# Background tasks cut into chains of small steps in an attention and gated-MLP kernel, with wo's splits and three sets of w_down's sums moved to chunk 1's projections

## The chip, the cores and the metric

The kernel runs on one core of one Trainium2 chip. The metric is the device time of one execution in microseconds; the time of the kernel before is the median of three runs. A profile of one more execution, with its trace, shows what each engine did: TensorE (PE, and PEld for its weight loads), VectorE (DVE), ScalarE (ACT), GpSimd (POOL) and SyncE (SP), whose in-order queue issues every DMA here.

## The reference

For x of 2048 x 1024, layer-normed to xn, the result is x + s * g. s is linear attention with learned feature maps and 32 heads of 32: phi is a pair of softmaxes (of p and of -p, with p = q w_phi or k w_phi), and

```python
kv = einsum("bhsf,bhsd->bhfd", phi_k, v)
z = einsum("bhsf->bhf", phi_k)
num = einsum("bhqf,bhfd->bhqd", phi_q, kv)
den = einsum("bhqf,bhf->bhq", phi_q, z)[..., None] + 1e-6
s = merge_heads(num / den) @ wo
g = silu((sigmoid(xn @ w_gate) * (xn @ w_up)) @ w_down)   # w_gate, w_up: 1024 x 3584
```

## The kernel before

Every large product is one level of a seven-product scheme on 2 x 2 blocks (names B11, T2, T3, B21, T1, T4, B22); the T operands are sums and differences of blocks, and results are formed by adding products in PSUM and in SBUF. Each operand is split into a high and a low part in the fast fp32 format (`split`: a ScalarE cast, L154, and a VectorE subtraction, L155), and each product is three matmuls (`mm3`, L159 to L161).

The 2048 rows go in two chunks of 1024. The stages, by the profile, are: chunk 0's projections V, K and Q (to about 300 us), chunk 0's GLU (to about 840), chunk 1's projections (to about 1078), chunk 1's GLU (to about 1650), the product with w_down (Down, to about 2170) and attention with wo (to the end). In a projection a group of four products (u = 0 to 3) goes to four banks, and `proj_out` evacuates them together. In the GLU there are 28 units of seven products, one bank each of 12 matmuls; the evacuations are L881 (B11, ScalarE), L883 (T2), L885 (T3), and L891 to L900 (B21, T1, T4, B22). Four banks go round; B21, T4 and B22 accumulate in the banks of B11, T3 and T1, so the evacuation of T3, say, must be over before T4 begins, one product later. In Down a step is eight banks of three matmuls (24 in all), 14 steps are one product of the scheme, and `evacuate` takes the eight banks at the end of it (L955 and L956 for B21, L973 for T4), through a ring `yr` of y buffers where the result is stored to g_d.

All else is background work, put between the products:

- `k_task(hb, t)`, 16 row tiles by 2 halves: load of k and v from qkv_d, `features` (row maxima and minima L451, L452, subtractions L460, L461, Exp L462, sums L464, reciprocal L465), L478, two splits, L489; then the products of phi and v (`kv_products`, L501). After each half come `kv_sum`, `kv_blocks` and `z_broadcast`.
- `q_features(t, hb)`: the same features for q, stored to e_d and r_d.
- `x_fetch`, `x_turn`: load, norm and transposition of chunk 1's rows.
- `wd_sums(j)`: four loads of w_down, four differences on POOL, four stores to wd_d (14 sets). `o_task(k)`: four loads of wo, four sums on POOL, seven splits stored to wo_d through three buffers (4 tasks).
- `q_task(t, hb)`, during Down: load of e_d (L635), multiplication by z on POOL, denominators on VectorE (L642 to L649), a second multiplication on POOL, four stores to f_d (L654). 32 tasks.

Each of these is one function that traces all its instructions at once. `background(anchor, tasks)` takes the next task from a queue; `tc.issue_after(anchor)` orders the task's instructions on the anchor's engine (VectorE, as the anchors are evacuations) behind the anchor. What lies on other engines is only ordered by the compiler's scheduler, which has priorities by program order. Where the tasks go is in the main loop: `bg_proj0` takes four k tasks beside Q of chunk 0, one per group; `bg_glu0` the rest of chunk 0's work at evenly spaced products (list `due`); `bg_proj1` six sets of sums beside V and K of chunk 1, and `late_k` five tasks beside its Q; `bg_glu1` all that is left, 25 of late_k's tasks, wo's four and eight sets of sums, and 16 q_features, mixed evenly over 188 products. In Down, 32 q_tasks are spread over 78 steps, and the loads of w_down's operands (L602) and of h_d (L608) are issued by `down_prep`.

Places in SBUF are numbered slots of two halves of 512 columns; 36 to 38 are block p, 43 to 46 block fb, 47 to 54 block fc.

## Time and profile before

| what | value |
|---|---|
| time, median of 3 runs | 2418.87 us (2418.68 to 2419.66) |
| time of the profiled execution | 2424.93 us |
| its span, first to last instruction | 2423.2 us |
| granted TensorE clock, mean | 0.995 |
| DVE, ACT, POOL busy | 67%, 41%, 50% |
| DMA, mean | 258 GB/s |

Busy times add up what each engine ran, and their shares are means over stages that differ. Matmuls are pipelined and their ends are modelled, so the number of matmuls in a stretch says more of TensorE's pace than its busy time does. A wait is put down to the event that came last before the waiting instruction started. Page lines such as "L885 DVE" name the line of the kernel; L154, L155 and L58 are helpers that many places call (L58 is POOL's piecewise sum, difference or product), and there the tile names tell the places apart (w, p, x, fb and so on; "stk" and "stq" are the small tiles of a k and a q task).

### The profile page before, as it was taken

Reading aid. Unit: us, or ns where it says so; the run is one execution under the profiler, and the core shown is the slowest. Engines: PE = TensorE matmul, PEld = TensorE weight load, DVE = VectorE, ACT = ScalarE, POOL = GpSimd, SP = SyncE. Lnnn points to the kernel's source line nnn. Section 1 sums busy time; section 2 is a strip of 40 time slices with the busy share of each in tenths; the row PEclk is TensorE's granted clock in tenths of the full one; section 3 lists DMA queues with packets and bytes.
Section 4 is the critical chain, followed back from the end, with each engine's and each line's share of the span. In section 5 each row is a group of like instructions: output and inputs, shape, how many; then the busy total and the mean of one; then the engine's idle time right before and its main releaser. Section 6 shows DMA issues by size and latency. Waiting matters only on the chain.

```text
span 2423.2 us, 32511 instructions
## 1 busy us (share of the span) xinstructions
PE 2356.5 (97%) x10728; PEld 1948.3 (80%) x10728; DVE 1630.7 (67%) x2341; ACT 1004.0 (41%) x1490; POOL 1212.1 (50%) x1394
## 2 busy tenths in 40 slices
PE   7999999999999999999999999999989999999998
PEld 5788887788888888888788777878878887888887
DVE  7434797677677764387857898765556675567775
ACT  6432354444454442235544454343333333345442
POOL 5630265867768463003434655353444545533766
PEclk9999999999999999999999999999999999999999
DMA  7775466888888698568898978788667766878664
GB/s 283 256 271 173 156 236 238 288 301 304 274 305 313 245 328 274 174 212 287 288 340 297 309 273 298 268 305 316 218 202 238 249 209 221 281 251 295 213 192 157
DMA packets 262329, 626.22 MB, mean 258 GB/s; under 512 B 37904, under 2 KB 58384, under 8 KB 257552
## 3 DMA queue, kind: packets, MB, share of 16 engines
q1 hardware_dynamic: 262160, 624.15, 74.8%
q8 instruction: 84, 1.38, 0.2%
q14 instruction: 85, 0.70, 0.1%
HBM read 374.47 MB, written 249.56 MB: 258 GB/s over the span
## 4 chain that ended last, share of the span: by engine, by line
PE 65%; DMA 9%; POOL 9%; DVE 8%; issue 6%; ACT 2%; SPq 1%; DVEq 0%; POOLq 0%; ACTq 0%
PE bank L159 21%; PE bank L160 21%; PE bank L161 21%; POOL fc L58 5%; POOL fb L58 2%; POOL x L58 1%; DMA wo_d<-p 1%; DMA fb<-w_down 1%; DVE w L155 1%; DVE p L155 1%; DMA out<-fc 1%; DMA fc<-e_d 1%; PE bank L501 1%; DMA wf_d<-x 1%; DMA f_d<-fc 1%
## 5 line engine op out<-in xcount | busy, mean ns | idle before, releaser
L159 PE MATMUL bank<-x,w 128*128 128x512 f32 x2352 | 910.3, 392 | 31.0 <-DVE fc L885 9.1
L160 PE MATMUL bank<-x,w 128*128 128x512 f32 x2352 | 918.0, 390 | 0.0
L161 PE MATMUL bank<-x,w 128*128 128x512 f32 x2352 | 909.6, 390 | 0.0
L58 POOL TENSOR_TENSOR fc<-fc 128x256 f32<-128x256 f32 x532 | 447.3, 871 | 598.5 <-DVE fc L900 217.2
L159 PEld LDWEIGHTS bank<-x,w 128*128 128x128 f32 x2352 | 442.8, 188 | 133.3 <-DVE fc L885 11.5
L155 DVE TENSOR_TENSOR w<-fa,w 128x512 fp32r<-128x512 f32 (+1 forms) x444 | 397.3, 898 | 225.1 <-ACT w L154 214.4
L161 PEld LDWEIGHTS bank<-x,w 128*128 128x128 f32 x2352 | 443.2, 188 | 93.2 <-DVE w L155 0.3
L160 PEld LDWEIGHTS bank<-x,w 128*128 128x128 f32 x2352 | 443.3, 188 | 90.7 <-DVE x L155 0.3
L154 ACT CAST w<-fa 128x512 fp32r<-128x512 f32 (+1 forms) x444 | 308.0, 698 | 487.2 <-PE bank L160 313.6
L159 PE MATMUL bank<-w,x 128*128 128x512 f32 x708 | 278.3, 393 | 6.3 <-ACT x L154 3.4
L161 PE MATMUL bank<-w,x 128*128 128x512 f32 x708 | 277.4, 393 | 2.9 <-DVE x L155 2.9
L160 PE MATMUL bank<-w,x 128*128 128x512 f32 x708 | 277.0, 391 | 0.0
L58 POOL TENSOR_TENSOR fb<-fa 128x256 f32<-128x256 f32 x112 | 104.8, 956 | 223.5 <-DMA fc<-qkv_d 131.4
L58 POOL TENSOR_TENSOR fb<-fb,fc 128x256 f32<-128x256 f32 x132 | 122.4, 947 | 186.7 <-DVE fc L900 186.5
L159 PEld LDWEIGHTS bank<-w,x 128*128 128x128 f32 x708 | 133.5, 189 | 36.1 <-ACT x L154 5.6
L161 PEld LDWEIGHTS bank<-w,x 128*128 128x128 f32 x708 | 133.5, 189 | 31.7 <-DVE x L155 4.8
L160 PEld LDWEIGHTS bank<-w,x 128*128 128x128 f32 x708 | 133.6, 189 | 26.7
L58 POOL TENSOR_TENSOR fb<-fb 128x256 f32<-128x256 f32 x116 | 111.7, 988 | 71.9 <-DMA fb<-w_down 35.6
L155 DVE TENSOR_TENSOR x<-fa,x 128x512 fp32r<-128x512 f32 x112 | 90.6, 809 | 76.9 <-ACT x L154 76.9
L154 ACT CAST w<-fb 128x512 fp32r<-128x512 f32 (+1 forms) x114 | 71.1, 625 | 130.3 <-PE bank L160 92.6
L154 ACT CAST x<-fa 128x512 fp32r<-128x512 f32 x112 | 69.5, 620 | 122.4 <-DMA fa<-wd_d 66.2
L58 POOL TENSOR_TENSOR fc<-fc,sa 128x256 f32<-128x256 f32 x128 | 105.6, 853 | 21.0 <-issue 20.1
(204 smaller groups left out, 2877.0 us busy)
## 6 DMA issues: line engine op xcount, KB each, us to landing
ws_d<-w SPq DMA_DIRECT2D x112, 512.0 KB, 4.4
w<-ws_d SPq DMA_DIRECT2D x112, 512.0 KB, 5.6
fa<-w_gu SPq DMA_DIRECT2D x84, 512.0 KB, 5.2
fa<-h_d SPq DMA_DIRECT2D x84, 512.0 KB, 5.2
fa<-wf_d SPq DMA_DIRECT2D x32, 1024.0 KB, 5.8
h_d<-fc SPq DMA_DIRECT2D x120, 256.0 KB, 4.2
h_d<-fb SPq DMA_DIRECT2D x76, 256.0 KB, 4.6
fc<-qkv_d SPq DMA_DIRECT2D x64, 256.0 KB, 4.6
```

Source lines behind the costliest of these rows:

```text
L58: self.engine.tensor_tensor(o[:, s], a[:, s], b[:, s], op=op)
L154: nc.scalar.copy(o[0], src)
L155: return nc.vector.tensor_sub(o[1], src, o[0].bitcast(F32))
L159: nc.tensor.matmul(o, a[0], b[0], start=first, stop=False, **kw)
L160: nc.tensor.matmul(o, a[0], b[1], start=False, stop=False, **kw)
L161: nc.tensor.matmul(o, a[1], b[0], start=False, stop=last, **kw)
L501: nc.tensor.matmul(kvb[g // 2][:, g % 2 * 256:g % 2 * 256 + 256], v[:, g].rearrange("p a f -> p (a f)"), ph[:, g].rearrange("p a f -> p (a ...
```

## The change

Each background function becomes a generator, with `yield` between its steps, and a class runs chains of them:

```diff
+class Steps:
+    def __init__(self, *tasks):
+        self.tasks, self.now = deque(tasks), None
+        self.left = self.total = sum(n for n, _ in tasks)
+    def step(self):
...
+        self.left -= 1
+        self.now[0] -= 1
+        over = next(self.now[1], self) is self
```

A k task is 8 steps, a q_features 5, an x task 7 (fetch and turn in one), a set of sums 2, a wo task 6, a q_task 5; kv_sum, kv_blocks and z_broadcast are 4, 6 and 5. In a k task, for example:

```diff
         nc.vector.tensor_reduce(mx, pv, axis=AX.X, op=ALU.max)
         nc.vector.tensor_reduce(mn, pv, axis=AX.X, op=ALU.min)
+        yield
...
         nc.vector.tensor_tensor(ev[:, 1], mn, pv, op=ALU.subtract)
         nc.scalar.activation(e, e, AF.Exp)
+        yield
+        if not query:
+            v = whole(38).rearrange("p (g a f) -> p g a f", g=8, a=2)
+            split((v[:, :, 0], v[:, :, 1]), vraw.rearrange("p (g f) -> p g f", g=8))
+        yield
```

The products of phi and v wait for one further call (`KV_WAIT = 1`). The small tiles of features get tags of their own for k and q, one buffer each in place of two shared. The tasks are dealt out anew:

```diff
+    early_k = Steps(*ks[:CTT])
+    late_k = Steps(*ks[CTT:])
+    p_again = (2, lambda: plain(block, "p", 36, 3, F32))
+    beside0 = Steps(*xs), Steps(p_again, *qs[:16])
+    beside1 = late_k, Steps(*wd[WD1:], *qs[16:])
+    proj1 = Steps(*os, *wd[:WD1])
-    def background(anchor, tasks):
+    def background(anchor, tasks, n=1):
         kv_products()
-        if tasks:
-            with tc.issue_after(anchor):
-                tasks.popleft()()
+        with tc.issue_after(anchor):
+            for _ in range(n):
+                tasks.step()
+
+    def paced(anchor, streams, products):
+        n = -(-sum(a.left for a in streams) // max(1, products))
+        for _ in range(n):
+            background(anchor, max(streams, key=lambda a: a.left / a.total))
```

with `WD1 = 3` in place of 6. In the projections, one step behind each of the four evacuations of a group:

```diff
             for u in range(4):
                 proj_out(c, what, i, u, pbank[u])
...
+                if c == 0 and what == Q:
+                    background(last_evac[0], early_k)
+                elif c and not (what == V and i in (B11, B21)):
+                    if what != Q and u < 3 and proj1.left:
+                        background(last_evac[0], proj1)
+                    elif what == Q and i not in (B11, B21):
+                        background(last_evac[0], late_k)
```

and in the GLU, for the product number m of a chunk (0 to 195), in place of the `due` lists:

```diff
+        if m > 1:
+            if c:
+                paced(v.ins, beside1, 191 - m)
+            elif early_k.left:
+                background(v.ins, early_k)
+            else:
+                kv_products()
+                paced(v.ins, beside0, 187 - m)
```

wo's tasks load into slots 47 and 52 (before: 43 and 44). In Down there are two streams of q_tasks, for even and odd t, each with its buffers (e in slot 50 or 51, the product with z in 52 or 47), one step of each behind each step's last split; the y ring gives up slot 47:

```diff
-    yr = Ring(halves(47, 48, 49))
+    yr = Ring(halves(48, 49))
...
+        e, ez = whole(50 + t % 2), whole((52, 47)[t % 2])
...
+    late = [Steps(*[(5, lambda t=t, hb=hb: q_task(t, hb)) for hb in range(2) for t in range(a, TT, 2)]) for a in range(2)]
...
+        if n < 2 * NJ * 3 - 2:
+            for a in range(2):
+                if late[a].left and (n or not a) and late[a].left > 5 * 16 * (80 - n) // 82 - 3 * a:
+                    with tc.issue_after(last_split[0]):
+                        late[a].step()
```

A q_task's steps are: the loads; the first multiplication; the denominators; the second multiplication; the stores to f_d.

More of the change, by code (lines that the diff above doesn't have):

```diff
@@ L39, in next @@
         return self.items[(self.n - 1) % len(self.items)]
+class Steps:
[3 more added lines that the diff above has]
+    def step(self):
+        if self.now is None:
+            if not self.tasks:
+                return
+            self.now = self.tasks.popleft()
+            self.now = [self.now[0], self.now[1]()]
+        self.left -= 1
+        self.now[0] -= 1
+        over = next(self.now[1], self) is self
+        assert over == (self.now[0] == 0)
+        if over:
+            self.now = None
 class Pieces:
@@ L298, in o_task @@
         pool.sub(a12, a12, a11)
[L299 to L300 removed]
+        yield
+        yield
+        keep(T2, a11)
+        keep(T3, a21)
+        yield
+        keep(T1, a22)
+        keep(B22, a12)
     o_r = Ring((36, 37, 38))
@@ L475, in k_task @@
         nc.sync.dma_start(vraw, qkv_d[V, t, hb])
-        r = features(f"k{t}{hb}", kraw, e_k)
+        yield
+        r = yield from features(f"k{t}{hb}", kraw, e_k)
+        yield
         e3 = e_k.rearrange("p (g d) -> p g d", d=DH)
@@ L491, in k_task, with kv_products @@
             nc.sync.dma_start(zk_d, zacc)
-        kv_due.append((t, ph, v))
+        kv_due.append([KV_WAIT, t, ph, v])
     kv_due = deque()
-    def kv_products():
+    KV_WAIT = 1
+    def kv_products(now=False):
         while kv_due:
-            t, ph, v = kv_due.popleft()
+            if not now and kv_due[0][0]:
+                kv_due[0][0] -= 1
+                return
+            _, t, ph, v = kv_due.popleft()
             for g in range(8):
@@ L628, in q_features @@
         nc.sync.dma_start(p, qkv_d[Q, t, hb])
-        r = features(f"q{t}{hb}", p, e, True)
+        yield
+        r = yield from features(f"q{t}{hb}", p, e, True)
         nc.sync.dma_start(r_d[t, hb], r)
@@ L982, in hedgehog_glu_kernel @@
     ND = len(dsteps)
-    late = [(t, hb) for hb in range(2) for n in range(CTT) for t in (2 * n, 2 * n + 1)]
+    late = [Steps(*[(5, lambda t=t, hb=hb: q_task(t, hb)) for hb in range(2) for t in range(a, TT, 2)]) for a in range(2)]
     for n, (i, j, cs) in enumerate(dsteps):
@@ L1004, in hedgehog_glu_kernel @@
         if n == 0:
-            assert not (bg_proj0 or bg_glu0 or bg_proj1 or bg_glu1 or kv_due)
-        if n and n * 32 // 78 > (n - 1) * 32 // 78 and late:
-            t, hb = late.pop(0)
-            if t == 0:
-                nc.sync.dma_start(zb, zb_d[hb])
-            with tc.issue_after(last_split[0]):
-                q_task(t, hb)
+            assert not any(a.left for a in (early_k, proj1, *beside0, *beside1)) and not kv_due
+        if n < 2 * NJ * 3 - 2:
[3 more added lines that the diff above has]
+                        late[a].step()
         if 40 <= n < 56 and n % 2 == 0:
@@ L1014, in hedgehog_glu_kernel @@
         if n == ND - 2 * NJ:
-            assert not late and len(WO[B21]) == 4
+            assert not any(a.left for a in late) and len(WO[B21]) == 4
             block("x1", 4, 4, F32R)
```

117 lines of the change are left out of this document (56 added, 61 removed).

## The prediction

> **What bounds the kernel now.** I read the page's busy totals first, then busy times by stretch (all matmuls, and those of L501 alone), then who waited for whom on TensorE, then the timelines around the longest waits. Columns of the stretches: length, busy time of PE, PEld, DVE, ACT and POOL with instruction counts, granted clock, DMA share, GB/s. The last three rows of the first fence are L501's alone.
>
> ```profile
> PE 2356.5 (97%) x10728; PEld 1948.3 (80%) x10728; DVE 1630.7 (67%) x2341; ACT 1004.0 (41%) x1490; POOL 1212.1 (50%) x1394
> 300.00:480.00 180.00, 174.93 (x782) 143.08 (x781) 143.68 (x201) 84.87 (x123) 126.91 (x131) 1.00 0.72 254
> 480.00:840.00 360.00, 360.00 (x1590) 298.10 (x1589) 259.32 (x389) 169.19 (x244) 254.36 (x299) 1.00 0.83 292
> 900.00:1020.00 120.00, 120.00 (x531) 99.37 (x530) 46.71 (x51) 32.38 (x39) 27.33 (x30) 1.00 0.70 239
> 1080.00:1650.00 570.00, 556.29 (x2508) 456.50 (x2507) 437.99 (x596) 265.04 (x360) 263.94 (x284) 1.00 0.85 299
> 1320.00:1500.00 180.00, 170.85 (x767) 138.50 (x767) 159.99 (x208) 84.24 (x104) 100.69 (x100) 0.99 0.84 290
> 1650.00:2170.00 520.00, 507.07 (x2212) 417.96 (x2211) 308.43 (x512) 180.07 (x310) 248.17 (x302) 0.99 0.72 239
> 300.00:480.00 180.00, 5.95 (x40) 5.37 (x40) 1.00 0.72 254
> 1080.00:1650.00 570.00, 24.86 (x176) 23.77 (x176) 1.00 0.85 299
> 1320.00:1500.00 180.00, 11.48 (x80) 10.68 (x80) 0.99 0.84 290
> ```
>
> TensorE is busy for 97% of the span, so only its lost time can be won. The undisturbed stretch 480 to 840 gives its pace: 360 us / 1590 = 0.2264 us from one matmul to the next. An L501 matmul (phi times v) has half the columns; its mean is 284 ns against 390, so I take 0.226 - 0.106 = 0.12 us.
>
> ```profile
> L160 PE MATMUL bank<-x,w 128*128 128x512 f32 x2352 | 918.0, 390 | 0.0
> L501 PE MATMUL bank<-p 128*128 128x256 f32 x256 | 36.4, 284 | 0.4 <-DVE p L155 0.3
> ```
>
> Lost time by stage is the length less the matmuls at that pace. Early in chunk 0's GLU (300 to 480): 180 - 742 x 0.2264 - 40 x 0.12 = **7.2 us**. Chunk 1's GLU (1080 to 1650): 570 - 2332 x 0.2264 - 176 x 0.12 = **21 us**. Down (1650 to 2170): 520 - 2212 x 0.2264 = **19.2 us**. Together 47 us; the opening and the last stage are not touched by the change. Who ended TensorE's waits in those three stages, in that order:
>
> ```profile
> PE bank L159 <- DVE fc L885: 3.6, 2, 2.3
> PE bank L159 <- DVE fc L885: 5.6, 4, 2.7
> PE bank L159 <- DVE fc L956: 6.8, 1, 6.8
> PE bank L159 <- DVE fc L973: 5.2, 1, 5.2
> ```
>
> All are VectorE evacuations of a bank that the next product needs. Why were they late? Rows of the timelines of VectorE, SyncE's queue and ScalarE around the long waits (start, length, then the idle time before it):
>
> ```profile
> 1382.12 1.21 DVE L461 TENSOR_TENSOR fc<-stk,fc 128x512 f32<-128x512 f32 x1
> 1383.25 0.67 DVE L885 TENSOR_TENSOR fc<-fc,bank 128x512 f32<-128x512 f32 x1
> ...
> 1469.61 1.22 DVE L464 TENSOR_REDUCE stk<-fc 128x32 f32<-128x1024 f32 x1 [2.46 <-ACT fc L462]
> 1470.75 0.68 DVE L885 TENSOR_TENSOR fc<-fc,bank 128x512 f32<-128x512 f32 x1
> ...
> 1804.48 1.78 SPq L654 DMA_DIRECT2D f_d<-fc  x4
> ...
> 1808.90 0.38 SPq L602 DMA_DIRECT2D fa<-wd_d  x1
> ...
> 1814.18 0.62 ACT L154 CAST x<-fa 128x512 fp32r<-128x512 f32 x1 [9.74 <-DMA fa<-wd_d]
> ...
> 2054.39 0.86 SPq L957 DMA_DIRECT2D g_d<-fc  x2
> 2060.38 1.35 DVE L973 TENSOR_TENSOR fc<-x,bank 128x512 f32<-128x512 f32 x2 [5.55 <-DMA g_d<-fc]
> ```
>
> At 1382 the last of a run of two background tasks' features stands in front of L885. At 1469 VectorE stands in its queue waiting for the task's Exp (L462), with L885 behind it. At 1804 f_d's stores, which need POOL's product, leave SyncE's in-order queue; the next task's load of e_d (L635) reuses their buffer and must wait for them to land, and wd_d's load (L602) stands behind it until 1808.90. ScalarE's queue then waits 9.74 us for that load, with the evacuation L955 behind the wait. At 2060 an evacuation waits for a y buffer whose store left at 2054.39.
>
> **The change part by part.**
>
> *Chunk 0.* The eight early k tasks become 64 steps: 28 places among Q's projections (four per product group) and 36 after GLU products, one each, where before there were whole tasks every fifth product. Nothing is added. A step puts at most two wide VectorE operations in front of an evacuation, about 2.3 us by the two 1.2 us rows above; a product lasts 12 x 0.2264 = 2.72 us and the evacuation 0.68, so a lone step rarely makes TensorE wait. After the Exp come other instructions before L464. Of 7.2 us I leave 1.5: **gain 5.7** (bounds 0 and 7.2). The products of phi and v come one call later (KV_WAIT), which nothing waits for before kv_sum. The 138 steps of x and q that follow are also one a product, in the stretch that lost nothing; they stay free.
>
> *Chunk 1's projections.* wo's four tasks (24 steps) and three sets of w_down's sums (6) take 30 of 36 places in V and K; before there were six sets of sums. New on VectorE and ScalarE there: 28 splits; on POOL, 4 tasks against 3 sets, nearly nothing; on SyncE's queue 24 MB in place of 12 (a task loads 1 MB and stores 3.5, a set moves 2). The fill row is 900 to 1020: VectorE 46.7 of 120 us, ScalarE 32.4, the DMA share 0.70. The splits cost here what they cost in the GLU now:
>
> ```profile
> L155 DVE TENSOR_TENSOR p<-fb,p 128x512 fp32r<-128x512 f32 x28 | 23.7, 859 | 21.0 <-ACT p L154 20.8
> ```
>
> 23.7 us beside an idle VectorE is hidden by TensorE's own work; without that cover it would cost all of it. Before these splits VectorE also stood 20.8 us for ScalarE's cast, 0.7 each, while three buffers go round to wo_d. Evacuations that queue behind such a wait have three other banks' time, 3 x 2.72 us, until TensorE needs theirs. The bounds are 0 and 20.8; near the bottom, **1.5 us lost**, as 900 to 1020 loses none now.
>
> *Chunk 1's GLU.* wo's splits leave (23.7 us of VectorE), but Q's places now take 20 k steps, 2.5 tasks, where five whole tasks went before, so 2.5 tasks more come here. Pacing changes more: 202 k steps and 102 others for 189 products, rounded up, is two steps a product for the first 115 and one for the last 74. Costs, summed over these rows:
>
> ```profile
> L489 DVE TENSOR_TENSOR fc<-fc 128x1024 f32<-128x1024 f32 x20 | 27.9, 1396 | 0.1
> L478 DVE TENSOR_TENSOR fc<-fc,stk 128x1024 f32<-128x1024 f32 x21 | 27.0, 1286 | 0.4
> L155 DVE TENSOR_TENSOR p<-fc,p 128x512 fp32r<-128x512 f32 (+1 forms) x51 | 52.6, 1032 | 6.2 <-ACT p L154 3.7 <-PE bank L543 2.3
> L464 DVE TENSOR_REDUCE stk<-fc 128x32 f32<-128x1024 f32 x21 | 25.5, 1215 | 15.5 <-ACT fc L462 15.5
> L461 DVE TENSOR_TENSOR fc<-stk,fc 128x512 f32<-128x512 f32 x21 | 18.2, 866 | 0.0
> L451 DVE TENSOR_REDUCE stk<-fc 128x16 f32<-128x512 f32 x20 | 13.5, 677 | 4.3 <-DMA r_d<-stq 2.9 <-DMA fc<-qkv_d 1.4
> ```
>
> (L461 stands for its twin L460 too, L451 for L452.) A k task: 1.40 + 1.29 + 2 x 1.03 + 1.22 + 2 x 0.87 + 2 x 0.68 = 9.1; neighbours overlap by 0.08 (1469.61 + 1.22 ends after 1470.75), ten of them: **8.3 us**, with a short reciprocal **8.5**. A q task is the features alone, L464 to L451 of these rows: 4.3, less overlap and with its reciprocal **4.1**. Foreground: five and a half evacuations of 0.6 (L885 above, less overlap) and three splits like wo's of 0.78 in seven products, 0.8 us a product. In the densest part (about products 52 to 117) two steps a product are 0.171 k and 0.13 q tasks: 1.45 + 0.53 + 0.8 = 2.8 us of VectorE a product, against 2.72 + 0.171 x 8 x 0.12 = 2.88 us of TensorE. So VectorE is filled to 97% there for some 190 us; then one step a product, about 60%. Now, 1320 to 1500 has 160 us of VectorE for 687 x 0.2264 + 80 x 0.12 = 165 us of matmuls, as dense, and loses 15 us in its lumps. Without lumps and waits on Exp I leave 9 us there and 3 for the 11 sets of sums that lead the list at once (before: 8, spread): **12 of 21, gain 9** (bounds: 18 gained, if only evacuations of the kind at 1469 mattered; 24 lost, below).
>
> *A page beside the trace.* The Trainium skill, "TensorE: Matmul & The Clock Gate", section "Part 1: The HAM clock gate", has the clock fall after an idle window of about 3.4 us, so by it the 2.7 us wait at 1469 costs only itself. The next row disagrees: the granted clock was 0.69 right behind it, 11 matmuls in 3.5 us where 15.5 fit, 1.0 us more. By the page the gain would be 1 us smaller.
>
> ```profile
> 1471.50:1475.00 3.50, 3.50 (x11) 2.79 (x12) 3.46 (x4) 1.94 (x3) 3.50 (x4) 0.69 1.04 409
> ```
>
> *Down.* A q task becomes five steps, one a down step (24 x 0.2264 = 5.4 us), in two streams with buffers of their own. f_d's stores are queued a step after the multiplication that they wait for, and e_d's next load a step after the stores. So what held SyncE at 1804 goes, and with it the 6.8 us and the slow matmuls behind it. The price: slot 47 goes to the second stream, and the y ring falls from six halves to four, so at B21 and T4 the fifth of eight evacuations waits for the first's store instead of the seventh. Unshown; bounds: nothing, if stores leave at once (TensorE needs bank 4 only 2.7 us into the next step), and the present 19 us again, if they still leave late. The store at 2054 was late because of f_d and e_d ahead of it, so I stand near the bottom: 5 us left, **gain 14**. A wait in VectorE's queue at L973, or in ScalarE's at L955, holds the splits of later steps behind it, which run some steps ahead of TensorE.
>
> Sum: 5.7 - 1.5 + 9 + 14 = **27 us**. The profiled execution took 2424.93 us (span 2423.2); the median is 2418.87, 6 us lower, and I take the gain off it unchanged: **2392 us**.
>
> **The rivals.**
>
> *The two-step stretch binds on VectorE (slower).* Beside POOL, two-input operations stretch:
>
> ```profile
> L461 DVE TENSOR_TENSOR fc<-stk,fc x32: 676/684/1222, 226.9 to 1581.7; 128x512 f32<-128x512 f32 x32
> L900 DVE TENSOR_TENSOR fc<-fc,bank 128x512 f32<-128x512 f32 x39 | 26.4, 678 | 19.3 <-PE bank L161 10.7 <-POOL fb L58 8.3
> ```
>
> At the long end (1.2 for each 0.7, in L460, L461, the splits and L489) a k task is 10.4, a q task 4.9, the foreground 0.96: 3.4 us a product, 0.5 over, for some 75 products: 37 us, with 8 elsewhere 45 in place of 21. Less 18 from the other stages: +6, **2425**. The point from which it is slower is (39 - 8) / 75 = 0.41 us a product over the 2.88. For it: the sums crowd at the front. Against: they end before much of the stretch. The Trainium skill, "SBUF — State Buffer", section "Who interferes with whom", says that a VectorE instruction with two SBUF inputs contends with a GpSimd instruction that reads SBUF, and one with a single SBUF input does not. L461's spread and L900's steady 678 ns (one input is a bank) agree.
>
> *The smaller ring keeps Down's loss.* The other gains stay: -13, **2406**. For it: the wait at 2060 was already one for the ring. Against: what made that store late goes.
>
> *The change doesn't do what it says.* Only a step's VectorE instructions are tied behind the product; ScalarE's, POOL's and the queue's are not, and steps may be compiled back to back. Lumps stay, ring and pacing eat what Down yields: **2418**.
>
> *Nearly all is recovered:* **2374**.
>
> **How the numbers follow.** Forecast 0.57 (its own range 2379 to 2408), smaller ring 0.14, VectorE binds 0.14, no effect 0.09, all recovered 0.06. The range leaves out most of the last and the upper half of the slower case: 2377 to 2421. A change within 0.2% (4.8 us) can't be told from none: faster 0.74, same 0.11, slower 0.15.
>
> **What would show it.** Right: L885 and L893 nearly gone from TensorE's waits, no wait behind L956; VectorE above 90% in about 1150 to 1420 and light afterwards. Wrong: TensorE losing more than 20 us there with VectorE full; L955 or L973 waiting for g_d; ScalarE's splits waiting for wo_d in 860 to 1000 with TensorE idle.

## The result, and the profile after

The kernel after takes **2398.81 us** (median of 4 runs, 2394.39 to 2404.23) against 2419.26 for the kernel before (4 runs, 2418.68 to 2420.41): a ratio of **0.9916, 95% interval 0.9894 to 0.9938**, 20.4 us less. Its profiled execution took 2404.23 us (span 2402.4), the slowest of its four; the span of the profiled execution before was 2423.2. So the two traces differ by 20.8 us. The four runs of the new kernel lie 10 us apart. Those of the kernel before lie 2 apart here, but 8 to 15 in the 11 to 23 runs beside each set of experiments. So a number read from one trace of either has to be held against a scatter of that size.

The line numbers have moved: `split` is L175/L176 (before L154/L155), `mm3` L180 to L182 (L159 to L161), POOL's helper L79 (L58), phi times v L547 (L501). In the GLU B11 is L954, T3 L958 (L885), B21 L964/L966 (L891/L893), L970 and L973 T1 to B22 (L897, L900); in Down B21 is L1020 (L956), T4 L1037 (L973). First the busy totals, then the stretches that the prediction used, all matmuls (the columns are those of the prediction).

```profile
PE 2348.1 (98%) x10728; PEld 1946.5 (81%) x10728; DVE 1632.3 (68%) x2341; ACT 1000.8 (42%) x1488; POOL 1201.5 (50%) x1394
...
300.00:480.00 180.00, 180.00 (x818) 149.99 (x817) 148.25 (x202) 88.37 (x128) 127.42 (x134) 1.00 0.72 256
480.00:840.00 360.00, 358.70 (x1580) 296.24 (x1580) 256.96 (x392) 171.16 (x244) 251.02 (x297) 1.00 0.83 291
900.00:1020.00 120.00, 120.00 (x531) 99.39 (x530) 56.72 (x68) 41.15 (x57) 40.61 (x48) 1.00 0.91 328
1080.00:1650.00 570.00, 554.49 (x2508) 455.80 (x2507) 430.07 (x575) 247.27 (x331) 260.44 (x280) 1.00 0.79 275
1650.00:2170.00 520.00, 518.79 (x2300) 429.66 (x2299) 322.43 (x538) 191.87 (x331) 251.85 (x305) 1.00 0.75 250
```

The work is the same: 10728 matmuls and 2341 VectorE instructions, as before. Early in chunk 0's GLU 818 matmuls run where 782 ran; in Down 2300 where 2212 ran. In chunk 1's GLU the number has not changed: 2508 and 2508.

The lost time of a stretch is reckoned as in the prediction: its length, less its matmuls at 0.2264 us, those of phi and v (L501, L547) at 0.12. For 300 to 480, for example, 180 - 770 x 0.2264 - 48 x 0.12 = -0.1 (48 of the 818 are L547's); a number within about 1 of zero means that nothing was lost, as whole matmuls are counted at the edges. In this table are all kernels of this study, microseconds lost in each stretch of one trace each, and the measured ratio to the kernel before on the same chip.

| kernel | 300 to 480 | 480 to 840 | 840 to 1080 | 1080 to 1200 | 1200 to 1440 | 1440 to 1680 | 1680 to 2160 | ratio (95% interval) |
|---|---|---|---|---|---|---|---|---|
| before | 7.2 | 0.0 | 0.1 | 1.7 | 11.1 | 7.5 | 19.0 | |
| after | -0.1 | 2.3 | 0.1 | 8.1 | 12.8 | -0.8 | 1.6 | 0.9916 (0.9894, 0.9938) |
| e1_lump_glu | 0.6 | 6.6 | -0.1 | 9.0 | 8.4 | 1.1 | 2.1 | 0.9944 (0.9931, 0.9956) |
| e2_lump_down | -0.1 | 4.8 | 0.1 | 3.8 | 10.5 | -0.9 | 4.3 | 0.9905 (0.9891, 0.9919) |
| e3_even | 0.0 | 2.3 | 3.1 | 8.4 | 7.4 | -0.6 | 4.1 | 0.9913 (0.9900, 0.9926) |
| e4_spread | -0.1 | 2.3 | -0.1 | 6.1 | 13.2 | 0.2 | 2.1 | 0.9904 (0.9887, 0.9922) |
| e5_even_spread | -0.1 | 3.2 | 2.4 | 6.1 | -0.5 | -0.9 | 3.0 | 0.9894 (0.9881, 0.9907) |
| e6_old_down | -0.1 | 2.5 | -0.1 | 6.1 | 10.7 | -0.9 | 18.8 | 0.9981 (0.9971, 0.9991) |
| e7_one_ez | 0.1 | 3.4 | 0.1 | 4.0 | 10.2 | -0.9 | 0.0 | 0.9912 (0.9898, 0.9927) |
| e8_wo_back | 0.0 | 1.8 | 0.1 | 0.3 | 19.5 | 11.0 | 1.2 | 0.9979 (0.9967, 0.9990) |
| e9_pairs | -0.1 | 2.7 | -0.1 | 6.5 | 10.7 | -0.8 | 3.2 | 0.9925 (0.9903, 0.9948) |
| e10_buffers | 0.0 | 2.3 | -0.1 | 3.3 | 10.7 | -0.7 | 27.7 | 1.0002 (0.9989, 1.0015) |
| e11_wo_back2 | 0.0 | 2.7 | -0.1 | 9.5 | 7.8 | 14.6 | 1.6 | 0.9989 (0.9970, 1.0008) |
| e12_all | 0.1 | 2.3 | 3.3 | 2.7 | 0.0 | -0.6 | 1.6 | 0.9883 (0.9861, 0.9906) |

From before to after: 7.3 won early in chunk 0's GLU and 2.3 lost later in it, nothing in the projections, 0.2 in chunk 1's GLU (20.3 and 20.1), 17.4 in Down. That is 22.6, beside the 20.8 between the spans.

Chunk 1's GLU has changed inside. Its three parts, before and then after:

```profile
1080.00:1200.00 120.00, 118.77 (x545) 97.70 (x544) 93.34 (x132) 62.93 (x89) 42.74 (x47) 1.00 0.80 282
1200.00:1440.00 240.00, 232.57 (x1042) 189.82 (x1041) 185.52 (x252) 113.01 (x147) 119.97 (x126) 1.00 0.88 311
1440.00:1650.00 210.00, 204.95 (x925) 168.98 (x925) 159.12 (x214) 89.10 (x124) 101.23 (x111) 0.99 0.84 294
```

```profile
1080.00:1200.00 120.00, 113.77 (x513) 92.68 (x512) 81.55 (x100) 40.87 (x56) 79.53 (x89) 1.00 0.90 316
1200.00:1440.00 240.00, 230.72 (x1045) 188.28 (x1044) 202.99 (x278) 115.65 (x150) 106.20 (x113) 1.00 0.81 279
1440.00:1650.00 210.00, 210.00 (x954) 174.84 (x953) 145.54 (x199) 90.75 (x126) 74.72 (x79) 1.00 0.71 246
```

The end of the stage is free now (954 matmuls for 925). The head is worse: POOL is busy for 79.53 us of 120 where it was busy for 42.74, and TensorE does 513 matmuls for 545. In the middle VectorE is busy for 203 of 240 us, 85%, and from 1264 on, to 1440, for 164.65 of 176 us, 94%. Next come the rows of who ended TensorE's waits in 1080 to 1440 (total, times, longest), and then what the three engines did around one place in the head: VectorE, POOL and ScalarE, each with the idle time before an instruction.

```profile
PE bank L547 <- DVE p L176: 3.2, 3, 1.8
PE bank L180 <- ACT fc L954: 3.0, 2, 1.7
PE bank L180 <- DVE fb L966: 2.5, 2, 1.8
PE bank L180 <- DVE fc L973: 2.3, 3, 1.4
PE bank L180 <- DMA w<-ws_d: 2.2, 2, 1.6
PE bank L180 <- ACT fb L964: 1.6, 1, 1.6
...
```

The largest row is not an evacuation: the products of phi and v (L547) wait for the splits of phi on VectorE. Up to 1200 the waits add up to 2.9 us behind ScalarE, 2.2 behind loads and 1.1 behind VectorE; from 1200 on they are 7.1 behind VectorE and 1.7 behind ScalarE.

```profile
1107.67 0.68 DVE L176 TENSOR_TENSOR w<-fa,w 128x512 fp32r<-128x512 f32 x1
1116.32 0.69 DVE L973 TENSOR_TENSOR fc<-fc,bank 128x512 f32<-128x512 f32 x1 [7.97 <-POOL fc L79]
```

```profile
1112.08 2.82 POOL L79 TENSOR_TENSOR fb<-fb 128x256 f32<-128x256 f32 x4 [1.54 <-DMA fb<-w_down]
1114.86 1.43 POOL L79 TENSOR_TENSOR fc<-fc 128x256 f32<-128x256 f32 x2
```

An evacuation at the head (L973, of T4) waits 7.97 us: it writes the buffer that POOL's product for T1 (L79, fc) still has to read, and that product ends at 1116.29. POOL had spent its time on w_down's sums (fb), for whose loads it waits in its queue. In 1080 to 1200 VectorE's waits for POOL add up to 18.4 us; in the kernel before they were 1.3. ScalarE has its own waits. The longest row of each in 1200 to 1440, after and then before:

```profile
ACT L497 <- DVE fc L496: 42.5, 9, 8.7
```

```profile
ACT w L154 <- PE bank L160: 23.5, 13, 3.4
```

After, ScalarE's Exp (L497) stands 42.5 us in its queue for VectorE's subtraction (L496), 44.7 with three short rows; before it was 23.7 (three rows, 11.1, 7.5 and 5.1). The evacuations L954 and L964, which appear among TensorE's waits above, are ScalarE's and come behind such waits, as its timeline in the head shows (1123.84 behind a cast, 1134.00 behind an Exp and the load of a table for the evacuation's sigmoid):

```profile
1122.89 1.04 ACT L175 CAST p<-fc 128x1024 fp32r<-128x1024 f32 x1 [8.19 <-DVE fc L520]
1123.84 0.58 ACT L954 COPY fc<-bank 128x512 f32<-128x512 f32 x1
...
1131.63 1.06 ACT L497 ACTIVATE fc<-fc 128x1024 f32<-128x1024 f32 x1 [6.68 <-DVE fc L496]
1132.71 1.28 ACT L964 ACT_TABLE_LOAD   x1
1134.00 0.60 ACT L964 ACTIVATE fb<-bank 128x512 f32<-128x512 f32 x1
```

Before, ScalarE's longest row was a wait for TensorE (the buffer of a split that a product still reads), which is a wait of an engine that is ahead.

### The profile page after: what moved, and what is told of

It reads as the page before. It is cut to its first block, busy times and chain, and to the rows that moved or that the text cites. A ratio compares the mean times of both kernels' runs of the same rounds, so it can differ in the third digit from the quotient of the medians.

```text
span 2402.4 us, 32573 instructions
## 1 busy us (share of the span) xinstructions
PE 2348.1 (98%) x10728; PEld 1946.5 (81%) x10728; DVE 1632.3 (68%) x2341; ACT 1000.8 (42%) x1488; POOL 1201.5 (50%) x1394
## 4 chain that ended last, share of the span: by engine, by line
PE 69%; DMA 10%; POOL 7%; DVE 6%; issue 5%; ACT 1%; SPq 0%; POOLq 0%; DVEq 0%; ACTq 0%
PE bank L180 23%; PE bank L181 23%; PE bank L182 23%; POOL fc L79 4%; POOL fb L79 2%; POOL x L79 2%; DMA fb<-w_down 1%; DMA r_d<-stq 1%; DMA fa<-w_down 1%; DMA wd_d<-fb 1%; PE bank L547 1%; DVE w L176 1%; DVE p L176 1%; DMA w<-ws_d 1%; DVE x L176 1%
## 5 line engine op out<-in xcount | busy, mean ns | idle before, releaser
L180 PE MATMUL bank<-x,w 128*128 128x512 f32 x2352 | 909.5, 391 | 14.7 <-DVE fb L966 3.8
L182 PE MATMUL bank<-x,w 128*128 128x512 f32 x2352 | 905.6, 390 | 0.0
L79 POOL TENSOR_TENSOR fc<-fc 128x256 f32<-128x256 f32 x540 | 466.8, 895 | 420.9 <-DMA fc<-e_d 110.6
L176 DVE TENSOR_TENSOR w<-fa,w 128x512 fp32r<-128x512 f32 (+1 forms) x444 | 395.3, 893 | 229.5 <-ACT w L175 207.8
L180 PEld LDWEIGHTS bank<-x,w 128*128 128x128 f32 x2352 | 441.5, 188 | 113.7 <-DVE fb L966 5.6
L175 ACT CAST w<-fa 128x512 fp32r<-128x512 f32 (+1 forms) x444 | 307.5, 698 | 507.0 <-PE bank L181 346.9
L182 PEld LDWEIGHTS bank<-x,w 128*128 128x128 f32 x2352 | 441.7, 188 | 91.6
L180 PE MATMUL bank<-w,x 128*128 128x512 f32 x708 | 278.9, 394 | 7.2 <-ACT x L175 4.3
L182 PE MATMUL bank<-w,x 128*128 128x512 f32 x708 | 278.2, 394 | 2.9 <-DVE x L176 2.9
L79 POOL TENSOR_TENSOR fb<-fb,fc 128x256 f32<-128x256 f32 x132 | 124.6, 964 | 196.4 <-DVE fc L973 195.8
L79 POOL TENSOR_TENSOR fb<-fa 128x256 f32<-128x256 f32 x112 | 99.8, 911 | 244.0 <-DMA fc<-qkv_d 129.5
L180 PEld LDWEIGHTS bank<-w,x 128*128 128x128 f32 x708 | 134.0, 189 | 36.7 <-ACT x L175 6.5
L182 PEld LDWEIGHTS bank<-w,x 128*128 128x128 f32 x708 | 133.8, 189 | 32.1 <-DVE x L176 4.8
L79 POOL TENSOR_TENSOR fb<-fb 128x256 f32<-128x256 f32 x108 | 96.5, 919 | 113.9 <-DMA fb<-w_down 109.2
L175 ACT CAST p<-fc 128x512 fp32r<-128x512 f32 x100 | 75.3, 757 | 168.2 <-DVE fc L520 78.1
L79 POOL TENSOR_TENSOR fc<-fc,sa 128x256 f32<-128x256 f32 x128 | 96.6, 784 | 97.3 <-issue 90.8
L176 DVE TENSOR_TENSOR x<-fa,x 128x512 fp32r<-128x512 f32 x112 | 94.4, 843 | 46.4 <-ACT x L175 46.2
L175 ACT CAST w<-fb 128x512 fp32r<-128x512 f32 (+1 forms) x114 | 71.1, 625 | 128.6 <-PE bank L181 90.2
```

The lines of the kernel that those rows point to most:

```text
L79: self.engine.tensor_tensor(o[:, s], a[:, s], b[:, s], op=op)
L175: nc.scalar.copy(o[0], src)
L176: return nc.vector.tensor_sub(o[1], src, o[0].bitcast(F32))
L180: nc.tensor.matmul(o, a[0], b[0], start=first, stop=False, **kw)
L182: nc.tensor.matmul(o, a[1], b[0], start=False, stop=last, **kw)
```

## The experiments

All kernels are the kernel after with the edit shown, and ran as it did, beside runs of the kernel before. Those had a median of 2421 to 2423 us there, not 2419.26, so ratios compare the kernels and times do so only roughly.

### Whole tasks in the GLU, at the new places

```diff
     def step(self):
...
+            if self.whole:
+                list(self.now[1])
+                self.now[1] = iter(range(self.now[0] - 1))
...
-    early_k = Steps(*ks[:CTT])
+    early_k = Steps(*ks[:CTT], whole=True)
```

and the same for late_k, both streams of chunk 0 and the second stream of chunk 1: each task is issued whole at the place of its first step, and its other places are empty.

> The changed kernel with its pacing, slots and streams, but each background task in the projections' Q places and both GLUs traced whole at the place of its first step (the places of its other steps stay empty); Down, and wo's splits beside chunk 1's projections, keep their steps. If small steps are what freed the evacuations in the GLUs (theory A), chunk 0's GLU loses about 7 us again in 300 to 480 and chunk 1's more than its 21, with L885's successor L958 and L966 long in TensorE's waits: some 10 to 20 us slower than the changed kernel, 2409 to 2419. If only where the tasks are put mattered (rival), it stays within 4 us of 2399.

Measured: 2410.04 us (2406.87 to 2413.59, 5 runs), ratio 0.9944 (0.9931, 0.9956). The two stretches of chunk 0's GLU:

```profile
300.00:480.00 180.00, 180.00 (x811) 149.05 (x810) 148.59 (x200) 87.72 (x127) 129.22 (x132) 1.00 0.73 254
480.00:840.00 360.00, 354.90 (x1561) 292.22 (x1560) 253.95 (x384) 161.49 (x236) 253.73 (x296) 1.00 0.82 289
```

Early in chunk 0's GLU 811 matmuls run, nearly as many as with steps (818) and far more than before (782). So it is not the smallness of the steps that frees this stretch. It is the new places, or another part of the change that this kernel keeps (KV_WAIT, the small tiles' own tags); these were not tried apart. Later, in 480 to 840, the lumps lose 6.6 us where the steps lose 2.3. In chunk 1's GLU they lose 18.5, no more than the kernel after in its own trace (20.1). The ratio lies 0.0028 higher than that of the kernel after, about 7 us, with intervals that just overlap; the trace places about 4 of it. By the ratio it comes to 2406 us, which lies between the two expectations.

### Down taken apart: steps, dealing, buffers

The change to Down has three parts: q_tasks in steps; the **dealing**, an even and an odd task begun right behind each other and then no new one for some steps, where before a whole task came every 2.44 steps; and a second buffer for the product with z, paid for by a y ring of four halves instead of six. Five kernels separate them.

Whole q_tasks at the new places, with the new buffers and ring:

```diff
-    late = [Steps(*[(5, lambda t=t, hb=hb: q_task(t, hb)) for hb in range(2) for t in range(a, TT, 2)]) for a in range(2)]
+    late = [Steps(*[(5, lambda t=t, hb=hb: q_task(t, hb)) for hb in range(2) for t in range(a, TT, 2)], whole=True) for a in range(2)]
```

> The changed kernel with each q_task in Down traced whole at the place of its first step (two tasks every five steps), with the two streams, their buffers and the ring of four y halves as they are. If the steps free SyncE's queue and the evacuations (theory A), Down loses 15 to 25 us again, with L1017's waits at B21 and T4: 2413 to 2424. If the second stream's buffers alone do it (rival: the load of e_d no longer waits for the stores of the task before), Down loses under 6 us: 2399 to 2405.

Measured: 2399.19 us (2399.00 to 2404.93, 4 runs), ratio 0.9905 (0.9891, 0.9919). Without steps nothing is given back that can be measured. The theory on which the prediction's term for Down rested, that f_d's stores must be queued a step later than the multiplication, falls here.

Down exactly as before (places, buffers, ring), all else as after:

```diff
-    yr = Ring(halves(48, 49))
+    yr = Ring(halves(47, 48, 49))
...
-        e, ez = whole(50 + t % 2), whole((52, 47)[t % 2])
+        e, ez = whole(50 + t % 2), whole(52)
...
+        if n and n * 32 // 78 > (n - 1) * 32 // 78 and late:
+            with tc.issue_after(last_split[0]):
+                list(q_task(*late.pop(0)))
```

> The changed kernel with Down as it was before the change: whole q_tasks one at a time every 2.44 steps, one buffer for the product with z, the y ring of six halves. If Down's gain is the work of Down's own edits, the waits at B21 and T4 come back and Down loses 15 to 20 us: ratio about 0.998. If it came from what lies ahead of Down (rival: another order compiled, another phase at Down's start), Down loses under 6 us and the ratio stays at 0.991.

Measured: 2416.32 us (2411.60 to 2424.82, 11 runs), ratio 0.9981 (0.9971, 0.9991). TensorE's waits in 1650 to 2160 show the two of the kernel before again, at the evacuations of B21 and T4 and with nearly the same lengths (they were 6.8 and 5.2):

```profile
PE bank L180 <- DVE fc L1020: 6.8, 1, 6.8
PE bank L180 <- DVE fc L1037: 4.9, 1, 4.9
```

Steps kept, one buffer and the ring of six (the first two hunks of the diff above):

> The changed kernel with one buffer (slot 52) for the product with z in both streams, and the y ring back at six halves; the steps of the q_tasks stay. If the second buffer freed Down, since whole tasks with two buffers lost nothing, Down loses 10 us or more again: ratio 0.995. If the dealing in pairs, or nothing of this, did it, Down loses under 5 us: 0.991.

Measured: 2398.58 us (2397.46 to 2401.74, 4 runs), ratio 0.9912 (0.9898, 0.9927). Nothing lost in Down: the second buffer wins nothing, and the smaller ring costs nothing here.

Whole tasks, one buffer, ring of six, so all as before but the dealing (e2's and e7's edits together):

> Down with whole q_tasks, one buffer for the product with z and six y halves, all as before the change, but dealt as now: an even and an odd task right behind each other, then three down steps without, instead of one task every 2.44 steps. If the dealing alone keeps the tasks' stores and loads away from the evacuations of B21 and T4 (theory D), Down loses under 5 us: ratio about 0.990. If whole tasks need the second buffer (rival), the product with z of the second task waits and Down loses 10 us or more: 0.995 to 0.998.

Measured: 2404.30 us (2399.49 to 2408.35, 6 runs), ratio 0.9925 (0.9903, 0.9948).

The old dealing with the new buffers and ring (the last hunk of e6 alone):

> Down with whole q_tasks one at a time every 2.44 steps as before the change, but with the second buffer for the product with z and the y ring of four, as now. If the second buffer alone frees Down (rival of theory D), it loses under 5 us: 0.990. If the dealing decides (theory D), the waits at B21 and T4 come back, longer for the smaller ring: 18 us or more lost, ratio 0.998.

Measured: 2423.63 us (2415.75 to 2428.08, 12 runs), ratio 1.0002 (0.9989, 1.0015). Here are Down's stretches of e6, e9 and e10, in that order:

```profile
1650.00:2160.00 510.00, 496.93 (x2169) 409.68 (x2168) 305.97 (x506) 177.89 (x306) 244.59 (x295) 0.99 0.72 239
```

```profile
1650.00:2160.00 510.00, 507.40 (x2238) 419.54 (x2237) 333.01 (x526) 187.93 (x322) 258.93 (x304) 1.00 0.75 247
```

```profile
1650.00:2160.00 510.00, 492.76 (x2131) 405.19 (x2130) 302.96 (x501) 174.48 (x301) 236.95 (x291) 0.98 0.71 234
```

e6 and e9 differ in the dealing alone: 69 matmuls in the same 510 us, 15.6 us, and the intervals of their ratios lie apart. e10 and e6 differ in buffers and ring alone: 38 matmuls fewer, 8.6 us lost; by the ratios it is 5 us, with intervals that just overlap. And e9 beside e7 shows what the steps add: 3.2 against 0.0 us lost, ratios that can't be told apart.

What does the dealing do? The waits of SyncE's queue in Down, from before, e6, e9 and after, one row or two of each:

```profile
SPq L654 <- POOL fc L58: 109.2, 28, 7.7
SPq L635 <- DMA f_d<-fc: 53.5, 37, 4.4
```

```profile
SPq L718 <- POOL fc L79: 110.8, 27, 8.1
```

```profile
SPq L698 <- DMA f_d<-fc: 57.3, 40, 4.6
SPq L721 <- POOL fc L82: 39.6, 21, 4.4
```

```profile
SPq L695 <- DMA f_d<-fc: 66.1, 43, 4.7
SPq L718 <- POOL fc L79: 27.2, 18, 5.6
```

(In e9 the lines stand three further down: L721 is L718.) f_d's stores at the head of the in-order queue stand 109 us for POOL's second product in the kernel before, 40 with the dealing alone, 27 with the steps too. The wait of e_d's next load for the stores to land is unchanged (53.5, 57.3, 66.1), so that half of the prediction's account was never the price. A row of POOL and three of SyncE's queue show the first half in e6:

```profile
1791.25 3.70 POOL L79 TENSOR_TENSOR fc<-fc,sa 128x256 f32<-128x256 f32 x4
```

```profile
1787.24 0.42 SPq L660 DMA_DIRECT2D fa<-wd_d  x1
1794.98 1.77 SPq L718 DMA_DIRECT2D f_d<-fc  x4
1796.85 0.39 SPq L666 DMA_DIRECT2D fa<-h_d  x1
```

The queue stands from 1787.66 to 1794.98, when POOL ends the product (1791.25 + 3.70), and every load of Down's operands is behind it. Whether it is the pairing that shortens this, or only that no task now begins beside the evacuations of B21 and T4 (single tasks began at steps 27 and 69, right there; the pairs begin at 25 and 26, 30 and 31, 65 and 66, 70 and 71), wasn't tried and stays open.

### Chunk 1's GLU: the crowd at its head, two steps a product, and the exchange of wo for sums

Steps spread evenly (about 1.6 a product over the whole stage, where after has two for 115 products and then one; the edit paces chunk 0's x and q steps evenly too):

```diff
+    even = {}
+
     def paced(anchor, streams, products):
-        n = -(-sum(a.left for a in streams) // max(1, products))
+        left = sum(a.left for a in streams)
+        total, all_products = even.setdefault(id(streams), (left, max(1, products)))
+        n = max(0, left - total * max(0, products - 1) // all_products)
```

> The changed kernel with the steps dealt evenly over the GLU's products (1.6 a product from first to last in chunk 1) in place of two a product for the first 115 and one for the rest. If chunk 1's GLU loses its time because two steps a product fill VectorE (theory B), the loss between about 1200 and 1450 falls from some 13 us to 4 and VectorE's busy share there from 95% towards 80%: 8 to 10 us faster than the changed kernel, 2389 to 2391. If it is the sets of sums at the head of the list, on POOL and on the DMA queue (theory C), the loss stays in 1080 to 1200 and the time within 4 us of 2399.

Measured: 2402.51 us (2400.31 to 2404.72, 4 runs), ratio 0.9913 (0.9900, 0.9926).

The 11 sets of sums mixed evenly among the 16 q_features instead of ahead of them:

```diff
+    mixed = [qs[16:][n] if kind else wd[WD1:][n] for _, kind, n in sorted(
+        [((n + 0.5) / (NJ - WD1), 0, n) for n in range(NJ - WD1)] + [((n + 0.5) / 16, 1, n) for n in range(16)])]
-    beside1 = late_k, Steps(*wd[WD1:], *qs[16:])
+    beside1 = late_k, Steps(*mixed)
```

> The changed kernel with the 11 sets of w_down's sums mixed evenly among chunk 1's q features in their stream, in place of all 11 ahead of them. Theory C (POOL and the queue crowded by the sums at the head): the 8 us lost in 1080 to 1200 fall to about 3, and the time by some 5 us, 2394. Theory B: VectorE gets the q features earlier and for longer, POOL's sums fall beside the two-step stretch and lengthen its operations; the time stays or rises by up to 6 us, 2399 to 2405.

Measured: 2399.50 us (2395.57 to 2408.94, 6 runs), ratio 0.9904 (0.9887, 0.9922).

Both together:

> Even dealing of the steps and the sums of w_down mixed among the q features, both together. With even dealing alone the dense stretch lost nothing after 1264 but 16 us went before it, 5.5 of them in a wait for ws_d's load. If the front's loss is the crowd of sums on POOL and on the DMA queue (theory C) and the dense stretch's is VectorE (theory B), the two add: chunk 1's GLU loses under 10 us instead of 21, ratio to before about 0.986. If the losses only move from one queue to another when steps are shifted (rival), the GLU keeps 15 us or more and the ratio stays at 0.990.

Measured: 2394.71 us (2394.34 to 2397.16, 4 runs), ratio 0.9894 (0.9881, 0.9907).

Neither alone shows a gain in its time. To judge the traces one needs their scatter: after, e2, e6, e7, e9 and e10 all have the same dealing in this stage and lose 20.1, 13.4, 15.9, 13.3, 16.4 and 13.3 us in it (1080 to 1680, from the table), 15.4 on average. e3 (15.2) and e4 (19.5) lie within that; e5 (4.7) lies far outside. What each alone leaves over is seen when the stage is cut at 1264, after the crowded sums (their last load is issued at 1246 in after, at 1242 in e3). Lost us in one trace each:

| kernel | pace | sums | 1080 to 1264 | 1264 to 1650 |
|---|---|---|---|---|
| the six, mean and range | two, then one | at the head | 6.8 (4.3 to 9.5) | 9.1 (7.5 to 10.9) |
| e4_spread | two, then one | mixed | 9.5 | 10.5 |
| e3_even | even | at the head | 14.8 | 0.9 |
| e5_even_spread | even | mixed | 5.3 | -0.2 |
| e12_all (below) | even | mixed | 1.9 | 0.5 |

The second part of after and of e3 (120 and 128 of the matmuls are L547's):

```profile
1264.00:1650.00 386.00, 377.80 (x1713) 311.75 (x1712) 310.19 (x422) 179.99 (x234) 132.69 (x136) 1.00 0.74 252
1264.00:1650.00 386.00, 385.00 (x1761) 321.19 (x1762) 319.39 (x438) 178.70 (x236) 137.15 (x137) 1.00 0.75 259
```

The even pace by itself takes away the loss from 1264 on, in all three kernels that have it. But with the sums at the head e3 loses about as much more ahead of 1264 (14.8 against 6.8), and there e5 and e12, which spread them, do not. What spreading the sums saves at the two-step pace can't be told: e4's 9.5 lies within the range of the six. In e3, the largest of TensorE's waits in 1080 to 1290:

```profile
PE bank L180 <- DMA w<-ws_d: 5.5, 1, 5.5
```

A product waits 5.5 us for an operand of its own from memory. Such waits take 1.6 to 5.5 us in 1080 to 1200 of after, e1, e2, e3, e6, e7, e9 and e10, with the sums at the head, and at most 0.3 in e4, e5 and e12. In e4 VectorE stays as full in the middle as after, and TensorE as slow; in e5 neither is so:

```profile
1200.00:1440.00 240.00, 231.40 (x1047) 189.70 (x1046) 200.88 (x268) 104.96 (x142) 124.33 (x133) 0.99 0.84 286
```

```profile
1200.00:1440.00 240.00, 240.00 (x1100) 199.91 (x1100) 191.72 (x252) 102.10 (x139) 114.08 (x122) 1.00 0.80 277
```

1100 matmuls in 240 us, nothing lost, with VectorE at 192 us instead of 201. ScalarE's waits in the same stretch of e5:

```profile
ACT w L175 <- PE bank L181: 32.4, 17, 5.7
...
ACT fc L497 <- DVE fc L496: 14.5, 5, 4.1
ACT fb L497 <- DVE fb L496: 11.9, 4, 3.7
...
ACT L497 <- DVE fc L496: 4.6, 3, 1.9
```

ScalarE's longest row is again a wait for TensorE, and Exp's wait behind VectorE is 31.0 us in these three rows, where after had 44.7. By itself that wait does not measure what TensorE loses: before it was 23.7, and in e3, which loses 7.4 us in this stretch, it is 34.7.

wo's four tasks put back into chunk 1's GLU, six sets of sums beside its projections as before:

```diff
-    WD1 = 3
+    WD1 = 6
...
-        a11, a12, a21, a22 = bs = halves(47, 52)
+        a11, a12, a21, a22 = bs = halves(43, 44)
...
-    beside1 = late_k, Steps(*wd[WD1:], *qs[16:])
-    proj1 = Steps(*os, *wd[:WD1])
+    beside1 = late_k, Steps(*os, *wd[WD1:], *qs[16:])
+    proj1 = Steps(*wd[:WD1])
```

> The changed kernel with wo's four tasks and three sets of sums back where they were: six sets beside chunk 1's projections, wo's tasks at the head of the second stream in chunk 1's GLU, and on slots 43 and 44 again. If the move relieves VectorE and the stores there (theory: 23.7 us of VectorE and 14 MB of stores in the GLU's first third), the GLU loses 8 to 15 us more, ratio 0.995 to 0.998. If the room that wo left was filled at once by the k tasks dealt two steps a product (rival), the GLU's loss stays within 4 us of 21 and the ratio within 0.002 of 0.991.

Measured: 2416.39 us (2411.69 to 2423.05, 12 runs), ratio 0.9979 (0.9967, 0.9990). In this kernel the splits of phi and of wo take turns in block p step by step and overwrite one another, which changes part of the operands of phi times v and of the product with wo; the instructions are as many and as long. A second way of putting wo back has none of that: its tasks stand in the k tasks' own chain, after the first three of them, with places of their own:

```diff
-        a11, a12, a21, a22 = bs = halves(47, 52)
+        kv_products(True)
+        a11, a12, a21, a22 = bs = halves(52, 53)
...
-    late_k = Steps(*ks[CTT:])
+    late_k = Steps(*ks[CTT:CTT + 3], *os, *ks[CTT + 3:])
```

with WD1 = 6 and proj1 as in e8.

> wo's four tasks in chunk 1's GLU again and six sets of sums beside its projections, with wo's tasks as steps in the k tasks' own chain (after its first three tasks, in slots 52 and 53), so that phi and wo's splits never hold block p together. If the move relieves the GLU (theory), it loses 8 to 16 us more than the changed kernel's 21: ratio 0.995 to 0.998. If the run before lost its time only because phi and the splits waited for each other in block p (rival), the loss stays within 4 us and the ratio within 0.002 of 0.991.

Measured: 2417.45 us (2412.04 to 2429.89, 12 runs), ratio 0.9989 (0.9970, 1.0008). Both lose 31 to 32 us in chunk 1's GLU, where the kernels with wo moved lose 15.4 on average: the exchange is worth some 16 us there. That includes a longer two-step stretch, as the stage then has 322 steps in place of 304. The ratios say the same: 0.9979 and 0.9989 against 0.9916 are 15 and 18 us. The largest row of TensorE's waits in 1080 to 1650 of e8:

```profile
PE bank L180 <- DVE fc L966: 9.5, 5, 2.9
```

VectorE's evacuations are late again. So, had wo stayed in this stage, steps at this pace would have lost 11 us more there than the kernel before.

### The best of the parts

Even pace and spread sums (e5) with one buffer and the ring of six (e7):

> Even dealing, sums mixed among the q features, and in Down one buffer for the product with z with six y halves. The run with the first two lost 4.6 us in Down, 2.1 in a wait at T4 behind a g_d store; the run with six halves lost 1.3 in Down. If that wait is the ring's, some 3 us come off the 2394.7 of the first two: ratio 0.988. If it is chance of the order compiled, it stays at 0.989.

Measured: 2395.04 us (2389.78 to 2397.79, 5 runs), ratio **0.9883 (0.9861, 0.9906)**, the lowest of all. TensorE in the middle of chunk 1's GLU:

```profile
1200.00:1440.00 240.00, 239.60 (x1094) 199.12 (x1093) 194.52 (x254) 102.32 (x140) 114.19 (x121) 1.00 0.81 278
```

Chunk 1's GLU now loses 2.1 us in all. Against the kernel after the ratio is 0.0033 lower, 8 us, but the intervals overlap: that it beats the kernel before is shown, that it beats the kernel after is likely and not shown. All three kernels with the even pace lose 2.4 to 3.3 us in 840 to 1080, where the others lose none. TensorE waits 1.4 to 1.7 us of it, near 865, for an evacuation by ScalarE (L461, B21 of a projection); why that one is late wasn't followed up.

## Why the prediction was right, and where it was not

The forecast was 2392 us, a gain of 27; the gain is 20.4, and 2398.8 lies within the forecast's own range. Its method, to read what each stage loses and ask what of that goes, held. Its terms held less well.

**Chunk 0's GLU, 5.7 won.** Measured: 7.3 won early, 2.3 lost later, 5.0 together. The size was right. The reason is half right: e1 shows that whole tasks at the new places lose only 0.6 early. What the steps themselves win, 4 us, lies in 480 to 840, which lost nothing before and was taken as free.

**The projections, 1.5 lost.** Measured: none. VectorE went from 46.7 to 56.7 of 120 us in 900 to 1020 and the DMA share from 0.70 to 0.91, and 531 matmuls ran in both. The cover that was named hid it all.

**Chunk 1's GLU, 9 won: the step that failed.** Measured: 0.2 in the two traces; 4.9 (20.3 less 15.4) when the six kernels with this dealing are averaged, against one trace of the kernel before. The working left 9 us to the two-step stretch and 3 to the sums. The first held. From 1264 on the six lose 9.1 on average; VectorE, reckoned at 97% of a product there, is at 94% of 1264 to 1440; and the even pace takes this loss away (e3, e5, e12).

The second was too small: ahead of 1264 the six lose 6.8 on average and the kernel after 9.5. The working gave the sums their price without a mechanism, and the rival that names them has VectorE's operations stretch. The trace shows another way: POOL has 79.5 of 120 us of work and waits for loads in between (1.54 us at 1112.08), and a product that an evacuation waits for runs only behind that (7.97 us at L973). VectorE is late by that; so ScalarE's cast waits 8.19 us for VectorE, with ScalarE's evacuation L954 behind it, for which TensorE then waits (1.3 us). How much of the head's loss comes this way is not shown. With the sums spread and the pace left as it was (e4) the head still loses 9.5; with both changed it loses 5.3 (e5) and 1.9 (e12), and the whole stage 4.7 and 2.1.

Nor did the working give the exchange of wo for sums a price of its own. It set wo's 23.7 us of VectorE against 2.5 more k tasks and counted the rest as pace; measured, the exchange is worth about 16 us (e8, e11), and without it the stage would have lost more than before the change. The slow matmuls behind the wait at 1469, 1.0 us, went with that wait: the granted clock in 1440 to 1650 is 1.00 after and was 0.99.

**Down, 14 won: the size near, the cause wrong.** Measured: 17.4. The working gave it to the steps (stores queued a step after the multiplication) and to the second buffer. By e2 and e9 whole tasks keep nearly all of it, by e7 and e10 the buffer wins nothing, and by e9 against e6 the dealing alone brings 15.6 us. The diff showed the new places, and the working did not ask where the old ones fell beside the two evacuations that waited.

**The rivals.** VectorE binding for 37 us did not come; single operations did stretch (below), but not all of them over 75 products. The smaller ring cost nothing under the new dealing (e7); under the old one it cost 8.6 us in one trace and 5 by the ratios, with the buffer that goes with it (e10, beside e6). There VectorE's and ScalarE's evacuations wait 12.8 us for g_d's stores, and 5.0 in e6. So that rival's mechanism can be seen, under a dealing that the change itself removed. That the change does nothing is ruled out. Nearly all recovered, 2374, was reached by no kernel: e12, the best, comes to 2391 by its ratio.

**The signs.** L956's successor is gone from TensorE's waits in Down, whose only row there now is 1.0 us; L885's (L958) does not appear among those of chunk 1's GLU. L893's (L966) is not gone. VectorE above 90% in 1150 to 1420 did not come either (220 of 270 us, 82%); only 1264 to 1440 shows it (94%). Of the signs for wrong none came: TensorE lost 13.5 us in 1150 to 1420 and not over 20; L955's and L973's successors (L1019, L1037) wait 3.5 and 3.1 us for g_d in Down, but no wait of TensorE's there is put down to them; and ScalarE's splits wait 26.0 us for wo_d in 860 to 1000, while TensorE loses nothing.

## What to carry to other kernels

In Down a background task in an in-order queue cost by where it began beside the foreground's deadlines, more than by its length: shift the places before cutting tasks into steps, and test the two apart. When work is dealt out, price each engine's queue by what stands behind the head of it, not by busy time alone: POOL, busy for 66% of the head, held an evacuation there for 7.97 us. And spread each kind of task over the whole stage, loads and POOL's sums as well as VectorE's steps: here either measure alone left the time as it was, and with both the traces show the gain, the times only likely. When two places lose time, cut the stage where one of them ends and count each part by itself.

## What the runs showed of the hardware

A VectorE subtraction with two operands from SBUF can stretch further than the prediction took (1.2 us for each 0.7). The splits of p in the kernel after (number, then least, median and greatest duration in ns, first and last start):

```profile
L176 DVE TENSOR_TENSOR p<-fc,p x100: 627/693/2692, 226.2 to 1631.8; 128x512 fp32r<-128x512 f32 x68, 128x1024 fp32r<-128x1024 f32 x32
```

The longest, at 1116.92, has 128 x 512 elements, so 2.69 us stands against a median of 0.69 for both shapes together; it began right behind the long wait at L973, with POOL in the midst of its sums. The evacuations, one of whose operands is a bank, stay at 0.676 us in the same stage on average, and none of this line's 84 in the whole run is over 0.69:

```profile
L973 DVE TENSOR_TENSOR fc<-fc,bank 128x512 f32<-128x512 f32 x40 | 27.0, 676 | 35.4 <-PE bank L182 11.5 <-POOL fc L79 9.3 <-POOL fb L79 8.0
```

One such row shows no cause, and none was looked for.
